# A stacked cross network on one core: the searched stream of row products starts 24 chunks earlier, with a new order table

## The chip, the cores and the metric

One Trainium2 chip, one core of it. The metric is device microseconds of one execution. The kernel has one launch; its inputs and outputs lie in the chip's memory.

## The reference: what is computed

```python
B, F, D, L = 16384, 26, 16, 6            # Din = F * D = 416
x = x0                                    # [16384, 416] bf16
for l in range(6):
    proj = einsum('bd,de->be', x, ws[l]) + bs[l]      # ws[l] is 416 x 416
    x = x0 * proj + x
```

Six layers, each a 416 x 416 product over 16,384 rows, a bias, a product with the input x0 and an addition of the layer's own input.

## The kernel before: tiles, order of the work, lines

**Tiling.** The 16,384 rows are 8 groups g of 2,048. Features lie on partitions and rows on the free axis. 416 = 3 x 128 + 32, so a job (g, l), which is layer l of group g, has three output tiles i = 0, 1, 2 of 128 features and a tail of 32. A tile has four chunks j of 512 rows; a chunk fills one of the eight PSUM banks. It contracts over 416: three weight blocks t of 128 features (`wm`) and one of 32 (`w3`). The four 32-feature pieces of a group stand under one another on the 128 partitions of `x3`, one strip of 32 for each chunk, in some groups rotated by DMA (`rotate`, L464).

**Two ways to do a chunk.** In the first jobs a tile goes through the whole array: three 128 x 128 products a chunk (`full`, L673), or the same split over four 32-column tiles (L667), then one 32-row product for each chunk, with the four of a tile on the four strips at once (`rows32`, L694 or, with 32 x 32 tiles, L688). From tile 1 of job (0, 2) on, the kernel uses **row products**: each 128-feature block is cut into four 32-row products on one of the four row strips of TensorE (L1129), and one more for `w3` (L1133). A chunk is then 4 x 3 + 1 = 13 row products, all of which add into one bank. Four chunks are in flight, one on each strip, and a chunk is handed from strip to strip. The program object (`Program.add`) sees that two strips write one bank in turn, so the first product on the new strip waits until the old strip's last is done.

**Tails.** The 32 features of up to three jobs are done together (`tails`, L700): 12 products of 128 x 32 a job (L720) and 4 of 32 x 32 (L708).

**Evacuation.** ScalarE (ACT) adds the bias and writes a chunk to SBUF (`evacuate`, L538, up to two banks at once; `evacuate_chunk`, L574, one bank). VectorE (DVE) multiplies by x0 and adds x for two chunks at a time (L547 and L552, or L586 and L594). Tails go by L640, L642 and L644, one in three by DVE alone (L636).

**What sets the order.** `replay` (L231) walks a string, `ORDER`, one letter for each visit of a strip: the letter says which of the open chunks, counted by age, the strip takes next; "|" is a batch of tails. It keeps planned times in slots, when a bank comes free (`READ`, `NEXT`, `BACK`), when the x that a chunk needs is written (`needs`, `SUMS`), and returns the row products sorted by planned start. `stream` (L1085) emits them in that order. On the chip nothing follows these times: each engine runs its own list in order, and semaphores hold it. The program part before the stream (L1159 to L1180) goes tile by tile. `two_tiles` (L1141) does the first two tiles of job (1, 0): it issues block t = 0 of both tiles, eight banks, while the eight banks' later inputs are being made, then finishes tile 0, then tile 1.

The order of the tiles at the change, from `items`: (1,0) tile 0, (1,0) tile 1, (0,1) tile 0, tails of (0,1) and (1,0), (0,1) tiles 1 and 2, (1,0) tile 2, (0,2) tile 0, and then the stream: (0,2) tile 1 and so on. In the stream are 131 tiles, 524 chunks and 44 jobs' tails in 15 batches.

The start of the stream before, and of the part that the change replaces:

```python
    s_lo = items.index(("tile", (0, 2), 1))
    for n, it in enumerate(items[:s_lo]):
        ...
        if mode[n] in ("FR", "F1"):
            full(g, l, i, banks, True, False, columns=items[n - 1][0] == "tails")
            rows32(g, l, i, banks, False, mode[n] == "F1")
        else:
            rows32(g, l, i, banks, True)
            full(g, l, i, banks, False, False)
```

**Loads.** SyncE (SP) issues the weights (L392, L401), the transposing loads of x0 (L411, L421) and the rotations (L466, L467) in program order.

Of the kernel before, what the change touches and what calls it, by code (L numbers as in the profile page):

```python
# [3 lines left out]
P = 128  # L4
CH = 512
T32 = 32
# [15 lines left out]
class Program:  # L22
# [179 lines left out]
READ, NEXT, BACK, SECOND, PAIR, TAILS, SUMS = 19, 56, 70, 110, 56, 220, 240  # L202
LETTERS = "ABCDEFGHIJKLMNOPQRSTUVWXYZabcdefghijklmnopqrstuvwxyz0123456789"
ORDER = (
    "ABCDMBCTZOELBaAjZSIfFiQPVKHYBCcTVIDSJATKBQLWBQXKNALCZQLWBQCbMRLWBITWBQPCZMLWRALSBQLCRIbCRAPeJYWH"
    "N|AWPJQGDQBDWNITCJnQCZTIWBLQWNALWBQXCNIDWZIDWJYTCRbIWBLQBSbINWHAVCTUBOQLBaTARaDQZOLUSBDUORbICJbA"
    "aVTMGBPYBWPIRaHAORDYKBXQKBTIWBDUOZITCZIOTFADeRYPCNIbWQFPK|ABPWAVKPQBCPQVKDAVePQBKfMRaHJAbSIBKTAZ"
    "SLcNHCBQXBSMLBaAOXZQKHMVSDBQOXBMKXAVKDQVKDBMebUJOHAVObIRCLQBSfJ|EODBTAOZACbVcPKFAeXRYGPBYWPRAKPQ"
    "BiLMRGDNACbNAaXNISHBYCTNYCbVISPFAePBUKDVQaDRIOXFAOXBAObVQGLBcCXNAePZIWTFASPBcKPRUGDNAWDNQXCJAbWR"
    "APSJYDaRUDSJUfOF|ITCRIODJAbSJATJCQDOBPcWJDIeVbQOFXAVODUKBXQKBTIBaLQCZTAOQZLWFPAWNDUCNTUBOTIBaLQN"  # L210
    "WALVCQXBOQLBaTINWDIVODUCNXAOJXAWJDUeYBXOIZHSUBTOIBbCMZDWIZTO|EBPWQBOLAVCPQVKfMFSDARWPANXCUNSDIBS"
    "XYBTKAReLMVSbIBKTAhSLYNHCBQXNCMLWBAaPQVKDQBaPBUKjMZSXEBSPAZKPQVHCBQWDMRKXBIWDVAOXJAWfYJTCQZOLEBW"
    "DcRCTMJWbERKP|ABPWQBKPAVCPQVKDANebUBKXQNaHJASXIBKTAhSLYNHCBQXNCMLWBAaXQNKHAZWTMBKDYRKXNAWDNQXBOQ"
    "BObIRWDQBOTICfZAXaRIPFCYPBaUPCMVaLBIWDVQCPRICfJAebJUSPFAaPQVGL|MBDSNAPKBAObRUGLBAeXNYKHVAWTJAKTY"
    "BLCYRWDRIOXBIWPBUOLRAKbBAWPZQCLRYCbNIWTBISPBYKPRAeDQVPKAJXCURCPQJaDIBafQVGPBMaXRIOH|ABTOAZKPQBKD"
    "BUPaAVKbQdCbMRWLEBWTARKPYBWDNQKDZISXBIOTBAOfRYKDZQLWBQKXARKXMBWLBQCPZAWbJQGDQZWPBIWPQBOLAVCPQVKj"
    "MFSDARWPANXCUNSLEBSDYRCTIBafIVOTE|BPWRALOBcDOZQKXBIDVaITCRIbBSYLBSIXNaALVOQDKBQXKBITBaQLVOADOZXA"
    "WJAXSJYDSJYXOFQDZOAXBOQXBOQLBaITVCQDSZMLWBIXSBQLOBIbCZQLCZITWBQLBaITNWALVCUTBSATNaIDJWYTBSPAdOXY"
    "SF|AODVPAKNYXCBQXaJcHORAPaRIHCBUbCRMLWBIWTBQKPVALWRMGDBQCbRMWLBAWbNAKPZUCXQJaPBIWPBcKPVAWLMRCLBQ"
    "XCRMLWFAWTBQCPZAaPJAWbJMSDZcPCNXYSF|AOTBPAaBYSPJUGDdQODJMbWBIXOdAXKNQHCBQWDMRCbJAaTVIODJAfaUBXSc"  # L220
    "NKHAZSXIBLCVYLSNEXCMBWPIBWLAVCXQBOTAdaPUBOLQVaHJAbCMZSLUBSLARKfARWLMBKDYRCPRIbWBQXJOALBaQVCPISXB"
    "ASPYVKHMBCbNQeDJMSXZIP|FCATBaQPBOIDaVIDSJYDSZMXGJTASBjMCNULCVITBeQLNWADaRXMCJDYSBQPaJAbWRAjSJUPG"
    "dQLOBAPSBYPCVIPSBIDSVYDKRAbeJMXGBXMCVIPSBcLORALiNAXOJQDCNUTBOAXBeQPaBYLOVALWdMTGBYfSVMLG|ABWPAVK"
    "PQBCPVQCPJAebVAWLNQaHBYOXBUOLAVKbMRGDBQWDMRKXAJCbQVOLEBaXABOTYVGLMRWDIBSXIBTKAZSLMBKDQZKXARWDQNX"
    "KBISXNADOBcWbBMSXIZGDRYCTZIWPBIWfNQGLB|AWPRAKPBUCPRUKDJAbeJQPWFICXBUPChMLWFAWTBQKPVAWLNQCLBQCbMR"
    "WDJMWDVISPFAObBUCPVQKfNALWBQWLNACbRMLCYJTWARLW|AJTMWDJUCTVICTJWADVaMTBaNIDKVYTOBAfaNQLVGMTCJMSDA"
    "BXa"
# [3 lines left out]
def replay(tails, events, needs, keep):  # L231
# [12 lines left out]
    size = [[3 + (r == tails[c]) if c < n - keep else 2 * (r == tails[c]) for r in range(4)] for c in range(n)]  # L244
    free, flight, begun, act = [0] * 4, {}, 0, 156
    banks = [(0, 0), (0, 1), (0, 2), (0, 3), (84, 4), (84, 5), (178, 6), (178, 7)]
    home, read, out, latest, due = {}, {}, [], [[]] * 4, list(events)
# [11 lines left out]
    for letter in ORDER:  # L259
        if letter == "|":  # L260
            now, m = min(free), due.pop(0)
            parts = [(f - now) // SLOT for f in free]
            at = now + max((f - now) % SLOT for f in free)
            over(at)
            on = at + 3 * SLOT * m + PHASE
            moved = [on + SLOT * k for k in parts]
# [27 lines left out]
        else:  # L294
            start = max(now, flight[c][1] + FENCE)
        assert flight[c][0] >> r & 1
# [10 lines left out]
def bass_standalone__cross_network_dcn__recsys_kernel(  # L307
# [202 lines left out]
    def evacuate(g, l, i, banks, js, step, vector=()):  # L510
# [21 lines left out]
        while a <= js[-1]:  # L532
            if step > 1 and a % 2 == 0 and a + 1 <= js[-1] and banks[a + 1] == banks[a] + 1:
                w = 2
            else:
                w = 1
# [143 lines left out]
    def rows32(g, l, i, banks, first, small=False, inner=False):  # L680
        src, stok = x3_src(g, l)
        ecols = slice(i * P, (i + 1) * P)
        for j in range(NJ):
            r, q = quad(g, l, j)
            if small:
                for c in range(NJ):
                    o = slice(c * T32, (c + 1) * T32)
                    add("pe", lambda h, q=q, j=j, r=r, c=c, o=o: h.matmul(  # L688
                        psum[o, banks[j] * CH:(banks[j] + 1) * CH],
                        w3[l][q, i * P + c * T32:i * P + (c + 1) * T32], src[q, :],  # L690
                        start=first, stop=not first, tile_position=(r * T32, c * T32)),
                        reads=stok + [("w3", l, r)], writes=[("ps", banks[j])])
                continue
            add("pe", lambda h, q=q, j=j, r=r: h.matmul(  # L694
                bank(banks[j]), w3[l][q, ecols], src[q, :], start=first and not inner,
                stop=not first and not inner,
# [360 lines left out]
    mode = {}  # L1057
    prev = None
    for n, it in enumerate(items):
        if it[0] == "tails":  # L1060
            prev = None
        elif prev is None:
            mode[n] = "FR"
            prev = n
        else:
            mode[n] = "RF"
            prev = None
    for n in list(mode):
        if mode[n] == "FR" and not (n + 1 in mode and mode[n + 1] == "RF"):
            mode[n] = "F1"  # L1070

# [13 lines left out]
    def stream(run):  # L1085

        chunks, due = [], []
        for it in run:
            if it[0] == "tails":
                due.append(it[1])  # L1090
            elif it[1] not in order[-3:-1]:
                chunks += [(it[1], it[2], j) for j in range(NJ)]
# [5 lines left out]
        for c, ((g, l), i, j) in enumerate(chunks):  # L1098
            pairs = [[place.get(((g, l - 1), t, k), -99) for k in (j, j ^ 1)] for t in range(NT)]
            needs.append([(t, *p) for t, p in enumerate(pairs) if c - max(p) < 30])  # L1100
        needs += [[]] * NJ
        plan, read, left = replay([quad(g, l, j)[0] for (g, l), i, j in chunks] + [quad(LAST, L - 1, j)[0] for j in range(NJ)],
                                  [len(b) for b in due], needs, NJ)
        at = list(ring)
# [4 lines left out]
        for _, r, c, b in plan:  # L1109
# [14 lines left out]
            t = seen[c, r] = seen.get((c, r), -1) + 1  # L1124
# [11 lines left out]
            if count[c] == 4 * NT + 1:  # L1136
# [4 lines left out]
    def two_tiles(g, l):  # L1141
# [17 lines left out]
    s_lo = items.index(("tile", (0, 2), 1))  # L1159
    for n, it in enumerate(items[:s_lo]):  # L1160
        if it[0] == "tails":
            tails(it[1])
            continue
        _, (g, l), i = it
        if (g, l) not in started:
            start_job(g, l)
        if n == 0:
            two_tiles(g, l)
            continue
        if n == 1:  # L1170
            continue
        banks = job_banks()
        if mode[n] in ("FR", "F1"):
            full(g, l, i, banks, True, False, columns=items[n - 1][0] == "tails")
            rows32(g, l, i, banks, False, mode[n] == "F1")
        else:
            rows32(g, l, i, banks, True)
            full(g, l, i, banks, False, False)
        evacuate(g, l, i, banks, list(range(NJ)), 2)
        finish_tile(g, l)  # L1180

    bka, left = stream(items[s_lo:])
# [158 lines left out]
```

## Time and profile before

| | us |
|---|---|
| median of 3 runs | 464.73 (464.65 to 465.34) |
| the profiled execution | 464.88 |
| its span | 463.1 |
| time outside the span in it | 1.8 |
| first product of job (1,0), L667 | 18.31 |
| first row product, L1129 | 40.48 |
| second batch of tails starts, L720 x36 | 57.96 |
| first product of the closing part, L1194 | 447.77 |

The profiled execution is one run, and the positions on the time axis are measured from its span's start. A row of the timeline has the start, the length of the merged row, the engine, the line of the kernel, the operation, its operands, the tile (rows * columns of the array), the shape and the number of instructions. Matmuls overlap: one of 512 columns is listed with some 374 to 380 ns, and the next on the same part of the array starts about 216 ns after it (24 products of L673 start at 31.96, the next kind at 37.24). So four row products on four strips take together what one product through the whole array takes.

### The profile page before, as it was taken

To read this page: it belongs to the slowest core of one execution; us is meant where nothing else is said; L and a number is where in the kernel's file an instruction comes from. 1 tells how busy PE (TensorE), PEld (TensorE's weight loads), DVE (VectorE), ACT (ScalarE), POOL (GpSimd) and SP (SyncE) were. 2 spreads that over 40 slices of the span, in tenths; PEclk is the share of its full clock that TensorE was granted. 3 is DMA by queue.
4 is the path that set the end of the run, shared out by engine and by line. 5 is a ranking of instruction groups with operands and counts; after the bars stand their busy time and mean duration, and the time that the engine had idled before them with its cause. 6 is when DMAs were issued, how large, how long until landed. Compare 5 with 4: busy or idle time off the path is not lost.

```text
span 463.1 us, 17845 instructions
## 1 busy us (share of the span) xinstructions
PE 458.4 (99%) x8001; PEld 266.7 (58%) x8001; DVE 403.2 (87%) x697; ACT 381.9 (82%) x609; POOL 7.7 (2%) x16
## 2 busy tenths in 40 slices
PE   9999999999999999999999999999999999999996
PEld 5444656575655656565665556566556565555552
DVE  2897898988889898898989989898988988989997
ACT  4686889887988889798888979888888888888786
POOL 1000000000000000000000000000000000000010
PEclk9999999999999999999999999999999999999999
DMA  8986859000002859089656965590000079172799
GB/s 233 194 168 142 152 125 191 10 23 9 19 4 36 138 184 192 16 129 219 91 90 127 208 98 91 101 234 24 24 4 4 24 139 299 47 124 52 209 161 314
DMA packets 136128, 53.79 MB, mean 116 GB/s; under 512 B 113642, under 2 KB 134644, under 8 KB 136052
## 3 DMA queue, kind: packets, MB, share of 16 engines
q1 hardware_dynamic: 135896, 52.54, 54.3%
q8 instruction: 62, 1.02, 0.9%
q14 instruction: 14, 0.11, 0.1%
q10 hardware_dynamic: 156, 0.11, 0.1%
HBM read 5.97 MB, written 13.63 MB: 42 GB/s over the span
## 4 chain that ended last, share of the span: by engine, by line
PE 96%; DVE 2%; ACT 1%; issue 0%; DVEq 0%
PE ps L1129 74%; PE ps L720 7%; PE ps L1133 6%; PE ps L673 4%; PE ps L667 1%; PE ps L708 1%; DVE x L1255 1%; DVE x L1249 1%; PE ps L800 1%; PE ps L818 1%; ACT tw L574 1%; PE ps L694 1%; DVE tw L586 0%; DVE x L594 0%; DVE x L1217 0%
## 5 line engine op out<-in xcount | busy, mean ns | idle before, releaser
L1129 PE MATMUL ps<-x,wm 32*128 32x512 bf16 x6288 | 372.8, 374 | 0.0
L574 ACT ACTIVATE tw<-ps,bias 128x512 bf16<-128x512 f32 x524 | 326.9, 688 | 48.8 <-PE ps L1129 35.9
L1129 PEld LDWEIGHTS ps<-x,wm 32*128 32x128 bf16 x6288 | 222.3, 92 | 135.1 <-ACT tw L574 6.4
L586 DVE TENSOR_TENSOR tw<-tw,x 128x1024 bf16<-128x1024 bf16 x262 | 176.7, 688 | 41.1 <-ACT tw L574 39.5
L594 DVE TENSOR_TENSOR x<-tw,x 128x1024 bf16<-128x1024 bf16 x262 | 171.2, 688 | 0.3
L1133 PE MATMUL ps<-x,w 32*128 32x512 bf16 x524 | 159.5, 374 | 0.0
L1133 PEld LDWEIGHTS ps<-x,w 32*128 32x128 bf16 x524 | 44.6, 92 | 5.9
L720 PE MATMUL ps<-x,wm 128*32 128x512 bf16 x564 | 33.6, 380 | 0.0
L640 ACT ACTIVATE ts<-ps,bias 128x512 bf16<-128x512 f32 x32 | 20.4, 685 | 13.1 <-PE ps L708 13.1
L538 ACT ACTIVATE tw<-ps,bias 128x1024 bf16<-128x1024 f32 (+1 forms) x24 | 20.7, 938 | 8.2 <-PE ps L694 7.0
L720 PEld LDWEIGHTS ps<-x,wm 128*32 128x32 bf16 x564 | 13.5, 96 | 18.2 <-ACT tw L574 3.7
L673 PE MATMUL ps<-x,wm 128*128 128x512 bf16 x92 | 21.3, 380 | 0.0
L644 DVE TENSOR_TENSOR x<-ts,x 128x512 bf16<-128x512 bf16 x47 | 18.4, 419 | 0.3
L547 DVE TENSOR_TENSOR tw<-tw,x 128x1024 bf16<-128x1024 bf16 (+1 forms) x21 | 13.0, 636 | 2.2 <-ACT tw L538 2.1
L673 PEld LDWEIGHTS ps<-x,wm 128*128 128x128 bf16 x92 | 8.3, 98 | 11.4 <-issue 2.1
L636 DVE SCALAR_TENSOR_TENSOR ts<-ps,bias,x 128x512 bf16<-128x512 f32 x15 | 11.2, 746 | 3.1 <-PE ps L708 3.1
L552 DVE TENSOR_TENSOR x<-tw,x 128x1024 bf16<-128x1024 bf16 (+1 forms) x21 | 12.6, 634 | 0.0
L642 DVE TENSOR_TENSOR ts<-ts,x 128x512 bf16<-128x512 bf16 x32 | 12.4, 417 | 0.0
L956 POOL COPY ost<-ot 128x512 bf16<-128x512 bf16 x5 | 4.6, 922 | 367.3 <-DMA ot<-x 367.3
L1194 PE MATMUL ps<-wm,x 128*128 128x416 bf16 x48 | 9.3, 340 | 0.0
L828 DVE COPY x<-ps 128x512 bf16<-128x512 bf16 x5 | 2.0, 422 | 8.2 <-PE ps L818 8.1
L1243 ACT ACTIVATE x<-ps 128x416 bf16<-128x416 f32 x16 | 7.7, 529 | 1.5 <-PE ps L1194 1.5
(52 smaller groups left out, 74.1 us busy)
## 6 DMA issues: line engine op xcount, KB each, us to landing
out_dram<-ost SPq DMA_DIRECT2D x6, 1664.0 KB, 8.3
x<-x SPq DMA_DIRECT2D x24, 96.0 KB, 2.2
x<-in_x_dram SPq DMA_DIRECT2D x8, 208.0 KB, 4.2
x<-in_x_dram SPq DMA_DIRECT2D x4, 416.0 KB, 8.1
wm<-in_ws_dram SPq DMA_DIRECT2D x5, 312.0 KB, 3.5
x<-x SPq DMA_DIRECT2D x22, 64.0 KB, 2.5
out_dram<-x SPq DMA_DIRECT2D x3, 416.0 KB, 2.6
out_dram<-ost SPq DMA_DIRECT2D x2, 416.0 KB, 2.8
```

The source lines that it names most:

```text
L538: add("act", lambda h, a=a, w=w, b0=b0: h.activation(tw[r][:, a * CH:(a + w) * CH], psum[:, b0 * CH:(b0 + w) * CH], ACT_F.Identity, bias=b ...
L547: add("dve", lambda h, a=a, e=e: h.tensor_tensor(tw[r][:, a * CH:e * CH], tw[r][:, a * CH:e * CH], x0s[s0][:, i * GC + a * CH:i * GC + e * ...
L552: add("dve", lambda h, a=a, e=e: h.tensor_tensor(xs[so][:, i * GC + a * CH:i * GC + e * CH], tw[r][:, a * CH:e * CH], src(i, a, e), ALU.ad ...
L574: add("act", lambda h: h.activation(tw[r][:, j * CH:(j + 1) * CH], bank(b), ACT_F.Identity, bias=bias[:, i, l:l + 1], scale=1.0), reads=[( ...
L586: add("dve", lambda h: h.tensor_tensor(tw[r][:, o], tw[r][:, o], x0s[s0][:, c], ALU.mult), reads=[("tw", r, k) for k in both] + [x0_tok(s0 ...
L594: add("dve", lambda h: h.tensor_tensor(paired(xs[so][:, c], "p (k j q) -> p j k q"), paired(tw[r][:, o], "p (j k q) -> p j k q"), paired(s ...
L640: add("act", lambda h: h.activation(ts[r][:, :], bank(b), ACT_F.Identity, bias=bias[:, 3, l:l + 1], scale=1.0), reads=[("ps", b), "bias"], ...
L644: add("dve", lambda h: h.tensor_tensor(x3s[so][:, :], ts[r][:, :], res, ALU.add), reads=[("ts", r)] + rtok, writes=[("x3", so), ("x3", so, ...
L673: add("pe", lambda h, t=t, j=j: h.matmul(bank(banks[j]), wm[l][:, t, ecols], src(t, j, j + 1), start=(first and t == 0), stop=(not first a ...
L720: add("pe", lambda h, t=t, j=j, src=src, l=l, b=b, ro=ro, qo=qo: h.matmul(psum[qo, b * CH:(b + 1) * CH], wm[l][:, t, NT * P:D], src(t, j, ...
L1129: add("pe", lambda h, l=l, t=t, j=j, b=b, q=q, ecols=ecols, src=src, kw=kw: h.matmul(bank(b), wm[l][q, t, ecols], src(t, j, j + 1)[q, :], ...
L1133: add("pe", lambda h, l=l, b=b, q=q, ecols=ecols, s3=s3, kw=kw: h.matmul(bank(b), w3[l][q, ecols], s3[q, :], **kw), reads=tok3 + [("w3", l ...
```

## The change

The tile-by-tile part shrinks to tile 0 of job (1, 0), and everything from (1, 0) tile 1 on goes through `stream`. These 24 chunks (six tiles) become row products, and the tails of (0, 1) and (1, 0) become a batch of the stream, with the 32 x 32 products behind the 128 x 32 ones. `two_tiles` issues block t = 0 for the four chunks of tile 0 and for two chunks of tile 1; those two are "begun" when the stream takes them over, and have 4 x 2 + 1 = 9 row products left in place of 13. Tile 0 is evacuated one bank at a time (`single`). Jobs (0, 1) and (0, 2) are walked by chunk pairs: chunks 0 and 1 of all three tiles, then chunks 2 and 3. `replay` gets new start times for the banks, and a time after a batch of tails before which a strip isn't to take its `w3` product (`TURN`, `SHIFT`), and `needs` is stricter by `LATE` slots for the first 36 chunks. The table ORDER is replaced as a whole. The modes F1 and inner go, and with them L688.

```diff
-READ, NEXT, BACK, SECOND, PAIR, TAILS, SUMS = 19, 56, 70, 110, 56, 220, 240
+READ, NEXT, BACK, SECOND, PAIR, TAILS, SUMS, SHIFT = 19, 56, 70, 110, 56, 220, 240, 215
+TURN, LATE = (200, 150, 260), 6
 ORDER = (
-    "ABCDMBCTZOELBaAjZSIfFiQPVKHYBCcTVIDSJATKBQLWBQXKNALCZQLWBQCbMRLWBITWBQPCZMLWRALSBQLCRIbCRAPeJYWH"
...
+    "ABCDERODNWDUJOQbBKbAbVSIDRKUDSJPUCJXASVLMCDNYWRLASJDYKBUbJCUTZKMHBaATZWIH|NCUCTBYCTVMaLBULRaHASZ"
...
-def replay(tails, events, needs, keep):
+def replay(tails, events, needs, keep, ahead, after):
-    size = [[3 + (r == tails[c]) if c < n - keep else ...
-    free, flight, begun, act = [0] * 4, {}, 0, 156
-    banks = [(0, 0), (0, 1), (0, 2), (0, 3), (84, 4), (84, 5), (178, 6), (178, 7)]
+    size = [[3 - (c < ahead) + (r == tails[c]) if c < n - keep else ...
+    free, flight, begun, act = [0] * 4, {}, 0, 243
+    banks = [(0, 0), (0, 1), (0, 2), (0, 3), (89, 4), (145, 5), (201, 6), (257, 7)]
...
+        if r == tails[c] and after[c][0] >= 0:
+            start = max(start, ons[after[c][0]] + after[c][1] - 3 * SLOT * (c < n - keep))
...
 def stream(run):
-                chunks += [(it[1], it[2], j) for j in range(NJ)]
+                if it[1] not in order[1:4:2]:
+                    chunks += [(it[1], it[2], j) for j in range(NJ)]
+                elif not it[2]:
+                    chunks += [(it[1], i, j) for a in (0, 2) for i in range(NT) for j in (a, a + 1)]
...
-            needs.append([(t, *p) for t, p in enumerate(pairs) if c - max(p) < 30])
+            needs.append([(t - LATE * (c < 3 * 3 * NJ), *p) for t, p in enumerate(pairs) if c - max(p) < 30])
...
+            begun = c < 2
+            whole = 4 * (NT - begun) + 1
-            kw = dict(start=count[c] == 1, stop=count[c] == 4 * NT + 1, tile_position=(r * T32, 0))
+            kw = dict(start=count[c] == 1 and not begun, stop=count[c] == whole, tile_position=(r * T32, 0))
...
 def two_tiles(g, l):
-        for i in (0, 1):
-            full(g, l, i, bks[i], True, False, ts_=[0], columns=True)
+        for i, chunks in ((0, range(NJ)), (1, range(2))):
+            full(g, l, i, bks[i], True, False, chunks=chunks, ts_=[0], columns=True)
         full(g, l, 0, bks[0], True, False, ts_=[1, 2], columns=True)
         rows32(g, l, 0, bks[0], False)
-        evacuate(g, l, 0, bks[0], list(range(NJ)), 2)
-        finish_tile(g, l)
-        rows32(g, l, 1, bks[1], False, inner=True)
-        full(g, l, 1, bks[1], False, False, ts_=[1, 2])
-        evacuate(g, l, 1, bks[1], list(range(NJ)), 2)
+        evacuate(g, l, 0, bks[0], list(range(NJ)), 2, single=True)
         finish_tile(g, l)
...
-    s_lo = items.index(("tile", (0, 2), 1))
-    for n, it in enumerate(items[:s_lo]):
...
-    bka, left = stream(items[s_lo:])
+    _, (g, l), i = items[0]
+    start_job(g, l)
+    two_tiles(g, l)
+    bka, left = stream(items[1:])
```

More of the change, by code (lines that the diff above doesn't have):

```diff
@@ new lines @@
+    "DJSUPGBAbVSMDBSYPVCMXRCIPRCcLaNEDaNUTCJQPaBIDVSIDBOYXBWQLZCbIROEDZODUJaTAKRcDJSAbRKUPBKUDRWIPBCY"
+    "NDWIDdSUbBKMXRaALNSYXFCQDZSIP|FCUPBWIDSVIDCVYSDRMbCNUbRCQLNaALBeUbKREDaRUPCJUDSVMDKNAbWJMTCJMDCZ"
+    "MTWJcDWRMLBKXARWDQBOTYJCITWZEDSVYDKNUTCJMTWBMLRCIDWBUPBOIXZQGDBUeTZEKPVAWL|QNCLOAJDBWcTNKALZCYXJ"
+    "OEDVaDUNKTYFCMTBaMLRCIDWRAPJSUDBOQbKBYTWBQLVCIThOEDZWDUNKTYFCMTBaMLRCAPWBUPJCULZCUTBeQLZWMHJAWDV"
+    "OQDNKAfJCYXRKALaQBTKYNHWAVP|QBOLRAKDBWYTNKALZCYXJOEDVaDUNKTYFCMTBaMLRCIDWRAPJSUDBOUbJCITZWEDVOYD"
@@ L228 @@
+    "QjJO|EDCVQODNIbFCDURCQPBeIbWRDQKNDYKVMTFCMDBiMbVSALROUDJOAbVKQPBCcPRWEDSBTYNCIDdSYXFOAPVeITFCYDV"
+    "SIPFCYDRWAPJCUbRCQLBeYLNWEDNWQLBKQDdSMLBKAnVSI|NHCUPBOAPBaPcVCULNSALZOUDNKQDJaQPFCMfRCMLBWIDBaUP"
+    "RKALZCUbJOEDVaPQFCYPBWIDVSIDRKUDBWMbRCMbKRALBWcTJaMDZUOLE|RCDQNCbAaTNIFWDUSDRICdDcWRbOEJXCRMDaNT"
+    "UOAB"
 )
-def replay(tails, events, needs, keep):
+def replay(tails, events, needs, keep, ahead, after):
     n = len(tails)
-    size = [[3 + (r == tails[c]) if c < n - keep else 2 * (r == tails[c]) for r in range(4)] for c in range(n)]
-    free, flight, begun, act = [0] * 4, {}, 0, 156
-    banks = [(0, 0), (0, 1), (0, 2), (0, 3), (84, 4), (84, 5), (178, 6), (178, 7)]
-    home, read, out, latest, due = {}, {}, [], [[]] * 4, list(events)
+    size = [[3 - (c < ahead) + (r == tails[c]) if c < n - keep else 2 * (r == tails[c]) for r in range(4)] for c in range(n)]
+    free, flight, begun, act = [0] * 4, {}, 0, 243
+    banks = [(0, 0), (0, 1), (0, 2), (0, 3), (89, 4), (145, 5), (201, 6), (257, 7)]
+    home, read, out, latest, due, ons = {}, {}, [], [[]] * 4, list(events), []
@@ L265, in replay @@
             on = at + 3 * SLOT * m + PHASE
+            ons.append(on)
             moved = [on + SLOT * k for k in parts]
@@ L508, in done_with, with evacuate @@
                 later.append(g + NX0)
-    def evacuate(g, l, i, banks, js, step, vector=()):
+    def evacuate(g, l, i, banks, js, step, vector=(), single=False):
         s0 = slot(g)
@@ L532, in evacuate @@
         while a <= js[-1]:
-            if step > 1 and a % 2 == 0 and a + 1 <= js[-1] and banks[a + 1] == banks[a] + 1:
+            if not single and step > 1 and a % 2 == 0 and a + 1 <= js[-1] and banks[a + 1] == banks[a] + 1:
                 w = 2
@@ L678, in full, with rows32 @@
                 after_chunk(j)
-    def rows32(g, l, i, banks, first, small=False, inner=False):
+    def rows32(g, l, i, banks, first):
         src, stok = x3_src(g, l)
@@ L684, in rows32 @@
             r, q = quad(g, l, j)
[L685 to L693, printed above, removed]
             add("pe", lambda h, q=q, j=j, r=r: h.matmul(
-                bank(banks[j]), w3[l][q, ecols], src[q, :], start=first and not inner,
-                stop=not first and not inner,
+                bank(banks[j]), w3[l][q, ecols], src[q, :], start=first, stop=not first,
                 tile_position=(r * T32, 0)),
@@ L1055, in finish_tile @@
             done_with(g, l)
[L1057 to L1070, printed above, removed]
     def nat_row(kk, j, b, first):
@@ L1099, in stream @@
             pairs = [[place.get(((g, l - 1), t, k), -99) for k in (j, j ^ 1)] for t in range(NT)]
-            needs.append([(t, *p) for t, p in enumerate(pairs) if c - max(p) < 30])
+            needs.append([(t - LATE * (c < 3 * 3 * NJ), *p) for t, p in enumerate(pairs) if c - max(p) < 30])
         needs += [[]] * NJ
+        turned = {job: (p, TURN[k] + SHIFT * (turn_of(job[0], 1) > 0))
+                  for p, b in enumerate(due) for k, job in enumerate(b)}
+        after = [turned.get((g, l - 1), (-1, 0)) for (g, l), i, j in chunks]
+        after += [turned[LAST, L - 2]] * NJ
         plan, read, left = replay([quad(g, l, j)[0] for (g, l), i, j in chunks] + [quad(LAST, L - 1, j)[0] for j in range(NJ)],
-                                  [len(b) for b in due], needs, NJ)
-        at = list(ring)
+                                  [len(b) for b in due], needs, NJ, 2, after)
+        at = ring[NJ:] + ring[:NJ]
         plan = [(t, r, c, at[b]) if r >= 0 else (t, r, [at[k] for k in c], b) for t, r, c, b in plan]
@@ L1135, in stream @@
                     reads=tok3 + [("w3", l, r)], writes=[("ps", b)], row=r)
-            if count[c] == 4 * NT + 1:
+            if count[c] == whole:
                 evacuate_chunk(g, l, i, j, b, read[c])
@@ L1158, in bass_standalone__cross_network_dcn__recsys_kernel @@
     add("pool", lambda h: h.memset(brow[:, :], 0.0), writes=["brow"])
-    s_lo = items.index(("tile", (0, 2), 1))
-    for n, it in enumerate(items[:s_lo]):
[L1161 to L1180, printed above, removed]
-    bka, left = stream(items[s_lo:])
+    _, (g, l), i = items[0]
+    start_job(g, l)
+    two_tiles(g, l)
+    bka, left = stream(items[1:])
     g, l = LAST, L - 1
```

38 lines of the change are left out of this document (15 added, 23 removed).

## The prediction

> **What bounds the kernel now.** I read the page first: the engines' busy shares, the clock, and the chain that ended last.
>
> ```profile
> span 463.1 us, 17845 instructions
> ...
> PE 458.4 (99%) x8001; PEld 266.7 (58%) x8001; DVE 403.2 (87%) x697; ACT 381.9 (82%) x609; POOL 7.7 (2%) x16
> ...
> PEclk9999999999999999999999999999999999999999
> ...
> PE 96%; DVE 2%; ACT 1%; issue 0%; DVEq 0%
> ```
>
> TensorE is the bound from end to end, at a full clock. DVE and ACT have slack everywhere on average, so what counts is how densely TensorE's own list is packed. There are two kinds of loss: a change of tile shape, and a strip that waits. The timeline of TensorE from the first product of job (1, 0) on shows the first kind:
>
> ```profile
> 18.31 3.62 PE L667 MATMUL ps<-x,wm 128*32 128x512 bf16 x64
> 21.87 0.61 PE L694 MATMUL ps<-x,w 32*128 32x512 bf16 x8
> 22.41 4.49 PE L673 MATMUL ps<-x,wm 128*128 128x512 bf16 x20
> 26.83 0.43 PE L688 MATMUL ps<-x,w 32*32 32x512 bf16 x16
> 27.06 0.42 PE L708 MATMUL ps<-x,w 32*32 32x512 bf16 x8
> 27.41 1.48 PE L720 MATMUL ps<-x,wm 128*32 128x512 bf16 x24
> 28.72 2.76 PE L667 MATMUL ps<-x,wm 128*32 128x512 bf16 x48
> 31.42 0.61 PE L694 MATMUL ps<-x,w 32*128 32x512 bf16 x8
> 31.96 5.35 PE L673 MATMUL ps<-x,wm 128*128 128x512 bf16 x24
> 37.24 0.61 PE L694 MATMUL ps<-x,w 32*128 32x512 bf16 x8
> 37.79 2.76 PE L673 MATMUL ps<-x,wm 128*128 128x512 bf16 x12
> 40.48 0.83 PE L1129 MATMUL ps<-x,wm 32*128 32x512 bf16 x12
> ```
>
> I call a "group" what fills the array once: one 128*128 product, four of 128*32, four of 32*128. 24 groups of L673 take 37.24 - 31.96 = 5.28 us and the 12 groups of L667 2.70 us. Subtracting, a group is 0.215 and the step to the next shape 0.1 longer. The single starts in the trace say it more finely: equal shapes follow each other by 216 ns, unequal ones by 304 to 318 in the switches of this stretch and of the 15 batches. So a **switch of shape costs about 0.097 us**.
>
> The second kind I read from the waits of the weight loads in the stream's first part, 40 to 62 us:
>
> ```profile
> PEld ps L1129 <- ACT tw L538: 0.7, 2, 0.4
> PEld ps L1129 <- ACT tw L574: 0.7, 3, 0.3
> ...
> PEld ps L1129 <- PE ps L1133: 0.2, 1, 0.2
> PEld ps L1129 <- PE ps L1129: 0.2, 1, 0.2
> ```
>
> These overlap with running matmuls, so I took them from the starts instead: on one strip the next row product starts after 216 ns, and all that is over this, divided by four strips, is lost array time. That is 0.53 us up to 62 us (for instance strips 0 and 3 start at 41.59 and 41.62 where 41.36 was due), 0.13 us from 62 to 240 and 0.24 us from there to 447. The stream is nearly full: there is at most 0.9 us of waiting left in it.
>
> **The change part by part.** Mark: the start of the second batch of tails (57.96 us), before which both kernels have done the same work but for one row product.
>
> *Groups.* Before, from 18.31: 16 + 2 + 20 + 1 + 1 + 6 + 12 + 2 + 24 + 2 + 12 = 98, and 311 row products = 77.75: together 175.75. After, in the emitted order: 56 products of L667 = 14, 4 of `rows32` = 1, 224 row products = 56, tails 6 + 1, 392 row products = 98: 176. No work is saved; the 24 chunks cost as much in strips as through the whole array.
>
> *Switches.* Before: L667 to L694, to L673, to L688, L708 to L720, L667 to L694, to L673, to L694, to L673, to L1129, and to L720 at the mark: 10. After: L667 to `rows32` (whose shape is the row products' own), row products to L720, L720 to L708, L708 to row products, and to L720 at the mark: 5. Five fewer by 0.097: **-0.48 us**. As a test of the counts: 175.75 x 0.216 + 10 x 0.097 + 0.53 = 39.46 against the measured 57.96 - 18.31 = 39.65.
>
> *Waits at the start of the stream.* The stream's cold start moves from 41 to 22 us. From the emitted order, with durations from rows: the two begun chunks have three products on their first strip and the two new ones four. A chunk that goes to another strip waits for the last product there: strip 0 took its at 41.59 where the old strip's last had started at 41.15, 0.44 later in place of 0.216. In the new order strip 1 takes over a begun chunk (0.22 idle), strip 0 takes one whose old strip ends one product later (0.44), strip 3 needs a bank of tile 0 that ACT frees 0.09 late: 0.75 / 4 = 0.19; one more hand-over, 0.05; two `w3` products of (0, 2) that wait for the x3 of the moved tails, 0.1; two banks, 0.04. Sum 0.38. The same reading of the old order gives 0.28, where 0.53 were measured. I take the difference of the readings, **+0.10 us**. Bounds: no wait at all, -0.53; twice the measured ones, +0.53.
>
> *The rest of the stream.* The new table replaces one that lost 0.37 us after 62 us. Followed in the same way, neither order shows a planned wait there, so I take 0, with bounds -0.37 (all go) and +0.37 (twice as many).
>
> *Evacuation.* Ten more ACT instructions, since pairs become singles. ACT does eight chunks in a row in 4.73 us (45.64 to 50.37), some 0.58 a chunk; 13 row products take 13 x 0.216 / 4 = 0.70. ACT is hidden by 0.12 a chunk. If that cover is gone for a stretch, it is the bank wait above. The Trainium skill (TensorEngine Tiling, PSUM Bottleneck) says that tiling speeds up TensorE and not the evacuation, which may become the bottleneck; at 0.58 against 0.70 it would not here, and the sum stays the same.
>
> *Moved loads.* SP's list keeps its order up to the first output store. The rotation of x3 that waits for the moved tails is reached by SP at 42.34 only; those tails, now at about 34, are written by about 38. Behind it stand weights 4 and 5 and group 3's loads, which therefore don't move. Weights 1 are issued at 17.26 and land some 3.5 us later (20.8); their first use moves from about 24 to 22.6, which leaves 1.8 us. Cost 0; bounds 0 and +0.5.
>
> *The end.* The closing part and its last dozen evacuations are the same list. It starts when the stream ends: 0, bounds -0.3 and +0.3 (half an evacuation more or less in the last burst).
>
> **Sum:** -0.48 + 0.10 = -0.38 us. Against the profiled execution, 464.88 - 0.38 = 464.5; that execution is 0.15 above the median of the runs, so **464.4 us** on the median. Differences under 0.2% (0.93 us) can hardly be told from no change here.
>
> **The rivals.**
>
> *B, faster: the waits go as well.* If the new table leaves no wait, -0.48 - 0.53 - 0.37 = -1.38: 463.4. For it: ACT, not the hand-over, ended most waits between 40 and 62, and the new start gives ACT its banks one by one. Against: the new order has a cold start too. Chance 0.25.
>
> *C, slower: hand-overs.* Each hand-over of a chunk between strips needs 0.44 us, and the table has to fill the gap with other chunks. There are 3 a chunk, so 72 or so come on top of 1572. Place: any strip whose next chunk isn't free. Price: 0.22 on one strip, 0.055 of the array. If the new table, searched for planned times, holds them worse on the chip and loses three times the 0.9 us, the time is 464.73 - 0.48 + 1.8 = 466.05. It decides the sign beyond 0.2% from 1.41 us of added waits on, 2.6 times the present ones. Against: the old table, made for the same chip, lost 0.37 us in 385. The Trainium skill (TensorEngine Tiling, Restrictions and Gotchas, Gotcha 1) says that different row tiles can't access one PSUM bank at the same time and that software has to synchronise; the 0.44 in place of 0.216 agrees, and by that rule more row products mean more such waits. Chance 0.13.
>
> *D, nothing:* the five switches are won at the start and lost again to the new cold start, 464.7. It would take 0.38 more of waits than I read. The emitted order shows that the switches do go. Chance 0.2.
>
> Forecast: 0.42. Forecast and D lie within 0.2%: 0.62; faster 0.25; slower 0.13. The range adds the bounds: low -0.48 - 0.53 - 0.37 - 0.1 gives 463.2; high -0.48 + 0.53 + 0.37 + 0.5 + 0.3 gives 465.9.
>
> **What would show it.** The second batch of tails at about 57.5 (18.31 before it unchanged): right for switches and start. Under 57.1 speaks for B, over 58.0 for D or C. From there to the end the two kernels should keep their distance: a distance that grows or shrinks by over 0.4 us is the table's doing. One step of shape from L667 until the first batch of the stream, no L673 after 18 us. It would be wrong if strips wait again and again after 62 us, or if ACT's busy rows show it late with banks until 60 us.

## The result and the profile after

| us | before | after |
|---|---|---|
| median, same chip (21 runs each) | 465.01 (464.65 to 465.59) | 465.91 (465.56 to 466.6) |
| ratio | 1 | 1.0019 [1.0013, 1.0025] |
| span of the profiled execution | 463.1 | 463.9 |
| first product of job (1, 0) | 18.31 | 18.17 |
| second batch of tails | 57.96 | 57.33 |
| first product of the closing part (L1194, now L1159) | 447.77 | 446.94 |
| issue of the last store | 460.86 | 460.30 |

The kernel became 0.9 us slower, where 0.4 us faster was forecast; the time lies 0.01 us above the upper end of the range. The ratio's interval excludes no change, though the difference is still inside the 0.2% that I called hard to tell.

The page of the changed kernel, in the lines that answer to those of before:

```profile
span 463.9 us, 18164 instructions
...
PE 457.7 (99%) x8157; PEld 264.8 (57%) x8157; DVE 404.8 (87%) x697; ACT 384.4 (83%) x619; POOL 7.6 (2%) x16
...
PEclk9999999999999999999999999999999999999999
...
PE 94%; DVE 4%; issue 1%; DVEq 0%
```

TensorE is a little less busy than before and the span is longer, at the same clock. More of the last chain lies on DVE. So whatever grew isn't matmul work. TensorE's timeline from the first product of job (1, 0) on (start, length, engine, line, operands, tile, shape, count):

```profile
18.17 3.19 PE L672 MATMUL ps<-x,wm 128*32 128x512 bf16 x56
21.30 0.40 PE L690 MATMUL ps<-x,w 32*128 32x512 bf16 x4
21.52 0.60 PE L1118 MATMUL ps<-x,wm 32*128 32x512 bf16 x8
...
34.05 1.48 PE L715 MATMUL ps<-x,wm 128*32 128x512 bf16 x24
35.46 0.41 PE L703 MATMUL ps<-x,w 32*32 32x512 bf16 x8
35.80 0.82 PE L1118 MATMUL ps<-x,wm 32*128 32x512 bf16 x11
```

The shape steps are the forecast ones, no L678 (the former L673) follows, and the stream runs from 21.52. Taken from the first product of job (1, 0), the second batch of tails comes after 39.16 us in place of 39.65 (-0.49), and the closing part after 428.77 in place of 429.46 (**-0.69**). The work of TensorE, DVE and ACT ends earlier: the last store is issued 0.56 us sooner. The loss is at the very end. From the closing part's first product to the end of the span it is 15.31 us before and 16.97 after, **+1.66**: the issue of the last store moves from 13.09 to 13.36 (+0.27), and from there to the end it takes 3.61 in place of 2.22 (**+1.39**). With the earlier start (-0.14), the sum -0.14 - 0.69 + 1.66 = 0.83 is the difference of the spans.

What lies behind the last issue is seen in the transfers of the last ten microseconds. First the kernel before, from 454 to 464 us (queues with packets, MB and share of the engines; then the issues, with the size of one and the time to its landing):

```profile
q1 hardware_dynamic: 1494, 2.83, 74.7%
...
out_dram<-x SPq DMA_DIRECT2D x3, 416.0 KB, 2.6
...
out_dram<-x SPq DMA_DIRECT2D x1, 104.0 KB, 1.7
```

The changed kernel, same stretch:

```profile
q1 hardware_dynamic: 1376, 2.64, 70.6%
q8 instruction: 1, 0.02, 0.6%
...
out_dram<-x SPq DMA_DIRECT2D x2, 416.0 KB, 4.9
out_dram<-x SPq DMA_DIRECT2D x1, 208.0 KB, 3.6
out_dram<-x SPq DMA_DIRECT2D x1, 104.0 KB, 3.1
```

The same stores, with fewer bytes left to move, take 1.4 us and more longer to land, and one packet of the queue "instruction" is new. Its totals stand in the queue table of the two pages, before and after:

```profile
q8 instruction: 62, 1.02, 0.9%
```

```profile
q8 instruction: 64, 1.05, 0.9%
```

The packets have 16,384 bytes each. The trace shows 16,025 instructions of TensorE before (8,001 matmuls, as many weight loads and 23 others) and 16,338 after; 62 x 256 = 15,872 and 63 x 256 = 16,128. So there is a packet for every 256 instructions, and the rest decides about one more: 16,025 leaves 153 and has none, 16,338 leaves 210 and has one. The Trainium skill (Runtime: NRT & Kernel Launch, Instruction fetch mechanics) says that instructions are refilled in 16 KiB blocks of 256 by the sequencer's own DMA queue, and that the cost of a boundary is mostly hidden. The counts agree; the last boundary here is not hidden.

A store counts as landed when 16 updates of its semaphore have come, and the trace lists each. Worked out from these, in us after the closing part's first product:

```
                          last packet   fourth last store    last store
                          starts        15th    16th         15th    16th update
before                      -0.45       13.22   13.23        14.81   14.82
after                       +9.32       13.59   15.32        15.09   16.49
```

After the packet one of the 16 updates of each store is late by 1.4 to 1.9 us (0.64 for the store that was under way when it started), and the other 15 aren't. The last store waits for that one.

### The profile page after: what moved, and what is told of

The parts are those of the page before. It is cut to its first block, busy times and chain, and to the rows that moved or that the text cites. A ratio compares the mean times of both kernels' runs of the same rounds, so it can differ in the third digit from the quotient of the medians.

```text
span 463.9 us, 18164 instructions
## 1 busy us (share of the span) xinstructions
PE 457.7 (99%) x8157; PEld 264.8 (57%) x8157; DVE 404.8 (87%) x697; ACT 384.4 (83%) x619; POOL 7.6 (2%) x16
## 4 chain that ended last, share of the span: by engine, by line
PE 94%; DVE 4%; issue 1%; DVEq 0%
PE ps L1118 75%; PE ps L715 7%; PE ps L1122 6%; PE ps L678 2%; PE ps L703 1%; DVE tw L591 1%; DVE x L1214 1%; DVE x L1220 1%; DVE x L599 1%; PE ps L795 1%; PE ps L813 1%; PE ps L672 1%; PE ps L690 0%; DVE x L649 0%; DVE ts L647 0%
## 5 line engine op out<-in xcount | busy, mean ns | idle before, releaser
L1118 PE MATMUL ps<-x,wm 32*128 32x512 bf16 x6568 | 389.2, 374 | 0.0
L579 ACT ACTIVATE tw<-ps,bias 128x512 bf16<-128x512 f32 x548 | 342.6, 687 | 49.1 <-PE ps L1118 34.4
L1118 PEld LDWEIGHTS ps<-x,wm 32*128 32x128 bf16 x6568 | 227.5, 92 | 144.1 <-ACT tw L579 4.9
L591 DVE TENSOR_TENSOR tw<-tw,x 128x1024 bf16<-128x1024 bf16 x274 | 185.4, 690 | 39.1 <-ACT tw L579 37.5
L599 DVE TENSOR_TENSOR x<-tw,x 128x1024 bf16<-128x1024 bf16 x274 | 179.6, 688 | 0.8
L1122 PE MATMUL ps<-x,w 32*128 32x512 bf16 x548 | 165.0, 374 | 0.0
L715 PE MATMUL ps<-x,wm 128*32 128x512 bf16 x564 | 33.6, 380 | 0.0
L715 PEld LDWEIGHTS ps<-x,wm 128*32 128x32 bf16 x564 | 13.5, 96 | 18.0 <-issue 3.5
L649 DVE TENSOR_TENSOR x<-ts,x 128x512 bf16<-128x512 bf16 x47 | 18.6, 420 | 0.4
L543 ACT ACTIVATE tw<-ps,bias 128x512 bf16<-128x512 f32 (+1 forms) x11 | 8.0, 808 | 4.1 <-PE ps L690 4.1
L1159 PE MATMUL ps<-wm,x 128*128 128x416 bf16 x48 | 9.4, 340 | 0.0
L678 PE MATMUL ps<-x,wm 128*128 128x512 bf16 x36 | 8.7, 380 | 0.0
L703 PE MATMUL ps<-x,w 32*32 32x512 bf16 x188 | 7.1, 385 | 0.0
L1159 PEld LDWEIGHTS ps<-wm,x 128*128 128x128 bf16 x48 | 4.2, 98 | 4.6 <-issue 1.5
```

Of the source, the lines that this page charges most:

```text
L579: add("act", lambda h: h.activation(tw[r][:, j * CH:(j + 1) * CH], bank(b), ACT_F.Identity, bias=bias[:, i, l:l + 1], scale=1.0), reads=[( ...
L591: add("dve", lambda h: h.tensor_tensor(tw[r][:, o], tw[r][:, o], x0s[s0][:, c], ALU.mult), reads=[("tw", r, k) for k in both] + [x0_tok(s0 ...
L599: add("dve", lambda h: h.tensor_tensor(paired(xs[so][:, c], "p (k j q) -> p j k q"), paired(tw[r][:, o], "p (j k q) -> p j k q"), paired(s ...
L649: add("dve", lambda h: h.tensor_tensor(x3s[so][:, :], ts[r][:, :], res, ALU.add), reads=[("ts", r)] + rtok, writes=[("x3", so), ("x3", so, ...
L678: add("pe", lambda h, t=t, j=j: h.matmul(bank(banks[j]), wm[l][:, t, ecols], src(t, j, j + 1), start=(first and t == 0), stop=(not first a ...
L715: add("pe", lambda h, t=t, j=j, src=src, l=l, b=b, ro=ro, qo=qo: h.matmul(psum[qo, b * CH:(b + 1) * CH], wm[l][:, t, NT * P:D], src(t, j, ...
```

## The experiments

Theories, in the letters that the expectations use. **F**: TensorE's last instruction packet falls among the last stores and holds up one of the 16 DMA engines; its place follows from the number of TensorE's instructions. Rivals: **N**, the number of packets counts, not their place; **D**, the end is late because DVE reaches the closing part late, through an idle stretch before the last tails (438.04 to 439.18 us). Later came **Q**, for the 0.3 us ahead of the last issue: GpSimd's copies beside DVE stretch DVE's instructions. The letters O, S, P and R are explained where an expectation uses them.

| run | median us | ratio [95%] | packets, last at | closing part: last issue, end |
|---|---|---|---|---|
| before | 465.01 | 1 | 62, -0.45 | 13.09, 15.31 |
| after | 465.91 | 1.0019 [1.0013, 1.0025] | 64, +9.32 | 13.36, 16.97 |
| e1_before_50more | 466.98 | 1.0038 [1.0025, 1.0050] | 63, +9.30 | 13.08, 16.94 |
| e2_before_86more | 466.56 | 1.0030 [1.0020, 1.0040] | 63, +7.19 | 13.08, 16.94 |
| e3_after_whole | 464.88 | 0.9991 [0.9982, 1.0000] | 63, +0.66 | 13.40, 15.63 |
| e4_after_whole_86more | 466.65 | 1.0029 [1.0017, 1.0040] | 64, +9.34 | 13.35, 17.38 |
| e5_after_146more | 466.03 | 1.0017 [1.0008, 1.0025] | 64, +1.17 | 13.40, 15.77 |
| e6_after_114more | 465.76 | 1.0017 [1.0006, 1.0028] | 64, +4.78 | 13.41, 15.83 |
| e7_after_86more | 465.94 | 1.0013 [1.0003, 1.0022] | 64, +5.09 | 13.41, 16.23 |
| e8_after_66more | 465.62 | 1.0018 [1.0009, 1.0028] | 64, +5.22 | 13.41, 16.34 |
| e9_after_flush | 466.18 | 1.0021 [1.0012, 1.0031] | 64, +9.24 | 13.38, 16.90 |
| e10_whole_flush | 464.67 | 0.9990 [0.9981, 0.9999] | 63, +0.91 | 13.18, 15.55 |
| e11_half_flush | 464.67 | 0.9989 [0.9980, 0.9998] | 63, -1.11 | 13.09, 15.32 |
| e12_whole_nocopy | 464.93 | 0.9995 [0.9986, 1.0005] | 63, +0.92 | 13.09, 15.48 |

Each ratio is to the kernel before on the same chip (medians 465.0 to 465.3). The last two columns are of one profiled execution each, in us after the closing part's first product. That of e6 is the fastest of its eleven runs (464.97; they scatter up to 467.41), so its columns don't show what its median lost.

### The packet, put into the kernel before

The warm-up matmuls on constants at the start (25 x 128 columns in 7 products) are cut into more and shorter products with the same number of columns (the diff has the 50 of 64 columns; the first run has 32 of 100), so that TensorE has more instructions and the same work; the stream and the closing part stay as they are.

```diff
-    keep_busy(25, 7)
+    one_ = nc.const_aps.tensor(1.0, [P, CH], BF16)
+    for k in range(25 * P // 64):
+        add("pe", lambda h: h.matmul(bank(7, n=64), one_[:, 0:P], one_[:, 0:64], start=True, stop=True), writes=[("ps", 7)])
```

> The kernel before with the 3200 columns of warm-up products ahead of the first data cut into 32 pieces of 100 columns in place of 7 of up to 512: 25 matmuls and as many weight loads more in TensorE's list (16,025 to 16,075 instructions), nothing else. Theory F (an extra 16 KB packet of TensorE's instructions is loaded while the last stores run, and holds up one of their 16 DMA engines): in the traces such a packet starts each time TensorE has passed 256 k + some 190 instructions. Before ends at 62 x 256 + 153, so none; this one ends at 62 x 256 + 203, some 13 past the mark, so there is one packet more, 63, after 456 us, and the time is 0.8 to 1.6 us longer, 465.8 to 466.6. Theory O (the loss at the end comes from the order of the closing list in the new table, the transposes and DVE's work): same time, 465.0 within 0.3, and 62 or 63 packets alike.

> The same with 50 pieces of 64 columns: 86 instructions more, 62 x 256 + 239, so the last packet should start some 50 instructions ahead of TensorE's end, about 454 to 456 us. Theory F: 63 packets, one of 16 updates of each last store late, time 466.0 to 466.8 (1 to 1.8 longer). Theory O: 465.0 within 0.3.

The second is the clean one. Its closing part starts at 447.83 (before 447.77) and issues its last store 13.08 after that (13.09); TensorE, ACT and DVE reach the end as before. Its transfers from 454 to 465 us:

```profile
q8 instruction: 1, 0.02, 0.5%
...
out_dram<-x SPq DMA_DIRECT2D x3, 416.0 KB, 4.9
...
out_dram<-x SPq DMA_DIRECT2D x1, 104.0 KB, 3.4
```

That is the picture of the changed kernel in the kernel before: the packet, 16th updates 1.25 us behind the 15th at the last store, an end at 16.94 in place of 15.31, and 0.30% more time. Of the 1.63 us at the end, the late update is 1.25; the other 0.40 is in all 16 (the 15th at 15.21 in place of 14.81), behind stores of which one was issued 1.1 us later (7.99 for 6.90), and its cause isn't shown. The first one shows the same end (16.94); its median, 466.98, lies above F's range; in its profiled execution job (1, 0) starts at 18.85 in place of 18.31.

### The packet, taken out of the changed kernel

The 14 groups of `two_tiles` go through the whole array in place of four column tiles: 84 instructions fewer (counting weight loads), 16,254 = 63 x 256 + 126. The fourth run adds the 86 of the warm-up again, which leaves 212.

```diff
-            full(g, l, i, bks[i], True, False, chunks=chunks, ts_=[0], columns=True)
-        full(g, l, 0, bks[0], True, False, ts_=[1, 2], columns=True)
+            full(g, l, i, bks[i], True, False, chunks=chunks, ts_=[0])
+        full(g, l, 0, bks[0], True, False, ts_=[1, 2])
```

> The changed kernel with the 14 groups of its first tiles as 14 products through the whole array in place of 56 of 32 columns: 42 matmuls and 42 weight loads fewer (16,338 to 16,254 = 63 x 256 + 126), and one switch of shape more behind the first tails (+0.1 us). Theory F: the 64th packet goes, the last one starts some 190 instructions before TensorE's end, ahead of the last stores, and the time falls by 1.3 to 1.6 us to 464.3 to 464.7, below the kernel before by 0.3 to 0.7. Theory O: 466.0, as the changed kernel, plus 0.1.

> The kernel of the run with whole products, and the warm-up cut into 50 pieces of 64 columns: the instructions come back (63 x 256 + 212), the shape stays whole. It parts the number of instructions from the shape. Theory F: 64 packets again, the last after 455 us, time back at 465.8 to 466.4. If the shape of the first tiles was what helped (theory S): as the run without the pieces. Theory O: 466.0 in both.

The transfers from 454 to 464 us without the packet:

```profile
out_dram<-x SPq DMA_DIRECT2D x3, 416.0 KB, 2.7
...
out_dram<-x SPq DMA_DIRECT2D x1, 104.0 KB, 1.7
```

And with it again:

```profile
q8 instruction: 1, 0.02, 0.6%
...
out_dram<-x SPq DMA_DIRECT2D x3, 416.0 KB, 5.0
...
out_dram<-x SPq DMA_DIRECT2D x1, 104.0 KB, 3.5
```

From last issue to end it is 2.23 us without the packet and 4.03 with it, at the same work; 1.63 of the 1.80 between them is the 16th update behind the 15th. The median without it, 464.88, lies 0.2 us above F's range. The stream from the first product of job (1, 0) to the closing part is 428.77, as in the changed kernel; the one more change of shape lies ahead of it, where the first product follows the start of the row before (L715) after 0.76 us in place of 0.66. The fourth run's start also lost time (its third transposing load of group 1 landed 0.85 us late, at 21.12), so its median holds more than the end.

### The packet, moved along

In the changed kernel the warm-up is cut further (80, 64, 50 and 40 products), which moves the last packet forward by the added instructions. All four have 64 packets, as the changed kernel has: F expects the loss to go, N expects it to stay.

> The changed kernel with its warm-up cut into 80 pieces of 40 columns: 146 instructions more on TensorE, everything else as it is. The list ends at 64 x 256 + 100, so there are 64 packets as in the changed kernel, but the last starts 168 instructions before TensorE's end, which in the changed kernel's trace was at 447.9 us, before the last stores. Theory F (what counts is where the last packet falls, not that it is there): no late updates, time 464.1 to 464.6, 0.5 to 0.9 below the kernel before, the stream's gain of 0.69 being left. Theory N (one packet more costs by itself): 466.0 or more. Theory O (order of the closing list): 466.0.

> The same with 64 pieces of 50 columns: the last packet starts 136 instructions before the end, about 450.1 us in the changed kernel's trace. Theory F: the packet is over before the last stores fill the DMA engines at some 452 us, so 464.1 to 464.8. Theory N and O: 466.0.

> The same with 50 pieces of 64 columns: the last packet starts 108 instructions before the end, about 450.8 us. Theory F: close to the edge; between 464.3 and 465.5. Theory N and O: 466.0.

> The same with 40 pieces of 80 columns: the last packet starts 88 instructions before the end, about 452 us, where the last stores have begun. Theory F: its DMA engine is late again, 465.2 to 466.2. Theory N and O: 466.0.

The mark came as F said: in e5 the 15th and the 16th update of the last store are 0.02 us apart, and from last issue to end it takes 2.37 us with all 64 packets, which speaks against N. But the expected times were missed in e5 to e7, where the medians lie nearer to N's 466.0, and none of the four is faster than the changed kernel beyond its interval. Other things were lost. The cut moves the earlier packets too, and in e5 one is at 19.43 us, among the loads of group 1:

```profile
18.86 2.33 PE L672 MATMUL ps<-x,wm 128*32 128x512 bf16 x40
21.78 1.05 PE L672 MATMUL ps<-x,wm 128*32 128x512 bf16 x16 [0.60 <-DMA x<-in_x_dram]
```

The third transposing load landed at 21.74 (20.27 in the changed kernel): 15 of its updates had come by 20.18, the last 1.56 us later. TensorE stood 0.60 us for it where the changed kernel has one unbroken row of 3.19 us. Job (1, 0) starts 0.69 us later there as well (18.86 for 18.17), which stays unexplained.

In e6 to e8 the last packet, at about 452 us, meets a store that was issued 2.3 to 2.7 us after the closing part's first product. One of its updates (two in e8) comes at 6.85 to 7.20, the others by 5.1 to 5.5. The last transposition, behind it, landed at 7.72 to 8.18 (7.06 in the changed kernel, but 7.67 in e5, with no packet near), and its store went out up to 1.1 us later (8.31 for 7.19). How much of that is the packet's is not shown. The four runs separate F and N by the profile of the end, not by the total time; the cut of the warm-up was too blunt for that.

### The 0.27 us ahead of the last issue

First, the idle stretch before the last tails: the tails' group is emitted right away in place of with the next.

```diff
+                if len(due) == 1:
+                    pr.flush()
                 tails(due.pop(0), corners_last=True, banks=c)
```

> The changed kernel with one addition to x let out ahead of the last batch of tails in DVE's list; in the changed kernel it is held back until the first tail instruction and DVE stands idle for 1.14 us (438.04 to 439.18), after which DVE is busy to the end and is the chain that ends last. TensorE's list is the same, 63 x 256 + 210 instructions. Theory D (the 0.3 us by which the closing part is longer in all kernels with the new table is DVE's late start on the last tails): from the first product of the closing part to the issue of the last store 13.0 to 13.1 us as in the kernel before, in place of 13.36 to 13.41; the last packet of instructions still comes after 456 us with one late DMA engine, so the time falls by 0.1 to 0.4 only, to 465.5 to 465.8. Rival P (the stretch is set by TensorE's products or ACT's last burst of eight): 13.4, 465.9.

> Both together: 14 whole products in the first tiles (63 x 256 + 126 instructions, no packet during the last stores) and the addition let out ahead of the last tails. Theories F and D: stream 0.69 shorter than before, closing part 15.3 us as before, time 464.2 to 464.6, 0.5 to 0.9 below the kernel before. F and P: 464.6 to 464.9. Neither: 465.9.

> As the run before, but only blocks 1 and 2 of tile 0 (8 of the 14 groups) whole: 63 x 256 + 162 instructions, the last packet some 230 instructions before TensorE's end, at 445 to 446 us. A check that the place of the packet counts and not the exact list: F and D 464.2 to 464.6 as the run before; if only the shape with no 32-column product helps, 465.5 or more.

Alone (e9) it brought nothing: 13.38 and 16.90. DVE is earlier on the last tails, but then it stands idle for 0.29 us at the start of the closing part, for a chunk that ACT ends 0.24 after its first product; so D falls as the cause. Together with the whole products (e10), or with two of the three blocks of tile 0 as whole products (e11, 159 instructions over a multiple of 256 in its trace), the time is the lowest seen, 464.67: 0.1% below the kernel before, with intervals that just exclude no change, and 0.3% below the changed one (0.9990 / 1.0019). That the idle stretch has a share in this is not shown, as e3 without that edit stands at 0.9991. In e11 the end is that of before to 0.01 us (13.09, 15.32); its profiled span is still 463.3, since its first product comes at 19.13.

Then DVE's timeline at the start of the closing part. Before (447.77 is the closing part's first product):

```profile
447.29 1.52 DVE L586 TENSOR_TENSOR tw<-tw,x 128x1024 bf16<-128x1024 bf16 x2
```

After (446.94), and GpSimd beside it:

```profile
446.64 1.29 DVE L591 TENSOR_TENSOR tw<-tw,x 128x1024 bf16<-128x1024 bf16 x2
447.85 1.49 DVE L599 TENSOR_TENSOR x<-tw,x 128x1024 bf16<-128x1024 bf16 x2
449.25 0.88 DVE L591 TENSOR_TENSOR tw<-tw,x 128x1024 bf16<-128x1024 bf16 x1
```

```profile
447.91 1.68 POOL L967 COPY ost<-ot 128x256 bf16<-128x256 bf16 x2 [27.05 <-DMA ot<-x]
```

The rows merge instructions. Taken one by one from the trace, start in us after the closing part's first product and length in us:

```
before   -0.48 0.68   0.35 0.69   0.96 0.68   1.56 0.69   2.16 0.68   2.88 0.69   COPY 3.49
after    -0.30 0.69   0.31 0.68   0.91 0.69   1.51 0.88   2.32 0.88   3.23 0.69   COPY 3.84
```

In the row of 1.52 no instruction is lengthened: between its two lie 0.15 us in which DVE waits for ACT, whose chunk ends at 0.32. The changed kernel starts the same instruction at 0.31, so it isn't late there. Then two instructions beside GpSimd's copies take 0.88 in place of 0.68, with no idle time behind them, and the copy (COPY) starts 0.35 later. Before, these copies (L972) ran at 443.85. They come later because SP issues the transposition that they wait for at 443.70 in place of 440.56. They lengthened two of DVE's instructions there too (0.88 at 444.36 and 0.77 at 445.28), but DVE's wait for ACT came behind these and hid it. The runs with the earlier tails fit this: behind the wait for ACT there are two lengthened instructions in e9 (last issue at 13.38), one in e10 (13.18) and none in e11 (13.09), where the copies run earlier. The last run leaves them out, in the kernel of e3, so 32 features of group 6 are missing from its output:

```diff
     def spread_pairs():
+        return
```

> The changed kernel with the 14 groups of two_tiles as whole 128 x 128 products, and without the two GpSimd copies that put the 32 tail features of group 6 into the output tile; so the tail features of that group are missing from the output. It is compared with the same kernel with the copies (464.88, 0.9991 of the kernel before; closing part: last store issued 13.40 after its first product, span ended 15.63). Theory Q (the copies run beside VectorE's pairs and stretch them, and this is the 0.3 that is left in the closing part): the first pairs of the closing part take 1.29 in place of 1.48 to 1.68, the last store is issued at 13.0 to 13.1, the span ends at 15.3, and the median is 464.5 to 464.7. Theory R (the 0.3 comes from the place where the stream hands the last evacuations over, or from TensorE): the last store stays at 13.36 to 13.41, the end at 15.6, and the median at 464.9.

DVE with the copies (e3):

```profile
447.15 1.68 DVE L591 TENSOR_TENSOR tw<-tw,x 128x1024 bf16<-128x1024 bf16 x2
```

And without (e12):

```profile
446.94 1.29 DVE L591 TENSOR_TENSOR tw<-tw,x 128x1024 bf16<-128x1024 bf16 x2
```

The stretch goes, and the last issue goes from 13.40 to 13.09, as Q said. So the copies do stretch DVE by 0.4 us here. The end only goes from 15.63 to 15.48, and the median doesn't follow (ratio 0.9995 against 0.9991 with the copies, intervals that overlap). That the 0.3 us are worth 0.3 us of the time is not shown. The Trainium skill (SBUF — State Buffer, Who interferes with whom) says that a DVE instruction with two inputs in SBUF contends with a GpSimd instruction that reads SBUF, over a shared port pair that is locked for one of them. The trace agrees in that such instructions lengthen, by 0.20 us each; how long either engine stood, it doesn't tell.

## Why the prediction was wrong, step by step

- **Groups and switches: right.** -0.48 for five switches, +0.10 for waits, -0.38 together; -0.49 measured from the first product to the second batch of tails. The one row product more (176 groups for 175.75) is 0.05 us that the sum leaves out.
- **Waits at the start: within the bounds, but of the wrong sign.** By the reading of the prediction (starts over 216 ns, divided by four) the stretch up to 62 us holds 0.48 in place of 0.53: -0.05, where +0.10 was forecast. With the row product, -0.48 - 0.05 + 0.05 is -0.48, beside the -0.49 measured. The changed kernel's waits of weight loads from 20 to 60 us put hand-overs first:

```profile
PEld ps L1118 <- PE ps L1118: 0.9, 6, 0.2
...
PEld ps L1118 <- ACT tw L579: 0.6, 3, 0.3
...
PEld ps L1122 <- DVE x L649: 0.4, 1, 0.4
```

  ACT's banks have become the smaller part and the one wait of a `w3` product for the moved tails (L649) is there, as read from the order.
- **The rest of the stream: better than forecast, within its bound.** Forecast 0, bounds ±0.37; measured -0.20. By the same reading the waits after 62 us fell from 0.37 to 0.16. So rival B's mechanism is partly real, and C's loss didn't come: there are more hand-overs and less waiting.
- **Evacuation and moved loads: right.** No wait for weights 1 and no growing queue for banks.
- **The end: this is the step that failed.** "The closing part and its last dozen evacuations are the same list … 0, bounds -0.3 and +0.3." The list is the same, its surroundings aren't: +1.66, of which 1.39 come from TensorE's instruction packet among the last stores and 0.27 ahead of the last issue, from two of DVE's instructions beside GpSimd's copies. I took the end to depend on when the stream finishes. It depends also on how many instructions TensorE has had by then: the change added 313 of them, which moved the rest over 256 from 153 to 210.
- **The rivals.** D ("nothing") forecast a loss in the cold start; the loss was at the other end. None of the rivals named the transfers at the end, so all the chances rested on TensorE's packing. Without the packet (e3) the kernel stands at 0.9991, which is 464.3 from the 464.73 of the forecast's base, beside the 464.4 forecast. That is partly luck: in e3's profile the stream gains 0.3 us more than the sum (0.69 for 0.38), and the end loses 0.3 where the sum has 0 (15.63 for 15.31).
- **The range.** Its terms add up to 464.73 + 1.22 = 465.95 at the upper end, where 465.9 was written, and the lower end takes 0.1 for the end, whose own bound was 0.3. The 0.01 us by which the time lies outside is rounding; a loss of 0.9 where a gain was forecast is not.

## What to carry to other kernels

Where a program ends on stores, look at how many instructions the busiest engine has. The "instruction" row of the queue table with packets of 16,384 bytes counts the loads of its instructions, one for every 256 here. One load among the last stores cost 1.4 us, more than the 0.69 us that the change saved in the stream. A step of 0.3% that no engine's timeline shows is looked for in the landings, update by update: one late of 16 suggests one DMA engine that had something else to do. A small change in the number of instructions (here 84, at unchanged work) is then a tool of its own, but it moves all the earlier loads as well. And a merged row of the timeline can hide a wait: its length is looked up instruction by instruction before an engine is called slow.

## What the runs showed of the hardware

- TensorE's instructions come in packets of 16,384 bytes, one for each full 256 instructions, which the profile counts on the same 16 DMA engines as the data. Their median is 0.97 to 1.08 us in the runs, and 0.92 to 0.96 us for those among the last stores. A rest of 100, 124, 126, 153 or 159 instructions brought none, a rest of 203, 208, 210, 212 or 239 one more. The packets among the last stores in after, e1, e2, e4 and e9 start when TensorE is 181 to 190 instructions past a multiple of 256; most others in these traces start later, up to the next multiple and past it.
- Such a packet makes one of the 16 updates of each later store late by 1.2 to 1.9 us (in after, e1, e2 and e4), more than its own time. Where the rest of the delay comes from stays open; the trace doesn't name the engine of a packet.
- A packet isn't only harmful at the end: at 19.4 us one update of a transposing load came 1.56 us behind the others (e5), and at about 452 us one or two of a store 1.5 to 1.9 us (e6 to e8).
- Two GpSimd copies of 128 x 256 lengthen two of DVE's two-input instructions (128 x 1024) beside them, from 0.68 to 0.88 us each (after, e3); without the copies it is 0.68 (e12).
